# Decode attention: a new order of work units, and cache chunks loaded and used in two halves

## The chip, the cores and the metric

The kernel runs on one core of a Trainium2 chip. The metric is the device time of one execution in microseconds (us). The kernel before takes 1149 us (1149.11 median of 3 runs, 1147.62 to 1150.12).

## The reference, cut to what matters

Two layers of attention, each followed by a small MLP block, run over a batch of 8 rows with one new token each. Both attention layers read the same K and V caches.

```python
B, Sq, D = 8, 1, 448;  Hq, Hkv, Sk, Dh = 16, 8, 4096, 256

def _A_ref(x, k_cache, v_cache, wq, wo):
    q = (x @ wq)...                              # 16 heads
    k = jnp.repeat(k_cache, 2, axis=1)           # two q heads share one kv head
    v = jnp.repeat(v_cache, 2, axis=1)
    scores = jnp.einsum("bhqd,bhkd->bhqk", q, k) * (Dh ** -0.5)
    o = jnp.einsum("bhqk,bhkd->bhqd", softmax(scores), v)
    return o... @ wo

x = x + _A_ref(_layernorm(x), K, V, wq, wo)      # pass 0
x = x + _B_ref(_layernorm(x), w1, w2, w3, w4)    # per row, no mixing across rows
x = x + _A_ref(_layernorm(x), K, V, wq, wo)      # pass 1, same K and V
x = x + _B_ref(_layernorm(x), w1, w2, w3, w4)
```

## The kernel before: the parts that matter

Work is cut into units (pass, batch row, pair of kv heads). A unit has four K chunks and four V chunks of 1 MB. SBUF holds 15 places of 1 MB. Eleven of a row's 32 chunks, those of head pair 3 and three of pair 2, are *kept*: they are loaded and transposed in pass 0 and stay until pass 1 uses them. So 424 chunks are loaded for 512 uses. While all eleven are kept, four places are left for everything else.

```python
NC = 15
kept = [(GP-1, kv, n) for n in range(4) for kv in range(2)] + [(GP-2, 0, n) for n in range(3)]
LAG = 4                                    # V chunk j-4 is used after K chunk j
keep, free = [2, 3], [0, 1]                # head pairs with kept chunks, and without
tasks = [(0, 0, gp) for gp in free + keep] + [(0, 1, gp) for gp in free]
tasks += [(0, 2, free[0])]
for b in range(Bn):
    tasks += [(1, b, gp) for gp in keep[::-1]]
    if b + 1 < Bn:
        tasks += [(0, b + 1, gp) for gp in keep]
    if b == Bn - 2:
        tasks += [(1, Bn - 3, free[-1])]
    tasks += [(1, b, gp) for gp in (free[:-1] if b == Bn - 3 else free)]
    if b + 2 < Bn:
        tasks += [(0, b + 2, gp) for gp in (free[1:] if b == 0 else free)]

def emit_loads(most=None):                 # called after each use: a free place is loaded again
    while loads and places and ...:
        it = loads.pop(0); p = where[it] = places.pop(0)
        ...
        nc.sync.dma_start(dst[:], src)     # one DMA, 128 partitions x 8 KB

def transpose_k(t):                        # 16 rows of 1 KB per partition, in place
    for half in range(2):                  # a half is half of every row
        w = t[:].bitcast(U32).rearrange("p (y e w) -> p y e w", e=2, w=64)[:, :, half]
        nc.vector.transpose(w, w)

def scores(sc, t, x, qbd, gp):             # 32 matmuls, four column groups (k) side by side
    kv = t[:].rearrange("p (k t e i r) -> p k e r t i", k=4, t=4, e=4, r=2)
    for n in range(8):
        ...
        for k in range(4):
            nc.tensor.matmul(sc[32*k : 32*k + 8, 128*x : 128*x + 128], ...)
```

Beside this stream runs the *chain* of a row: softmax sums, output projection, MLP and the new q, cut into 30 small steps that are spread over the items between the row's last pass-0 unit and its first pass-1 unit.

Of the kernel before, what the change touches and what calls it, by code (L numbers as in the profile page):

```python
# [10 lines left out]
U32 = mybir.dt.uint32  # L11
# [6 lines left out]
def kernel(  # L18
# [27 lines left out]
    nc = tc.nc  # L46
    Bn, Sq, D = A_x.shape
# [13 lines left out]
    NC = 15  # L61
# [58 lines left out]
    sc_t = [ps_s.tile([128, 512], FP32, name=f"sc{n}") for n in range(2)]  # L120
# [337 lines left out]
    def claim(st):  # L458

        return st.setdefault("begun", 0) == 0 and st.update(begun=1) is None  # L460

    def last(b, st):
        yield from half(st["o"], st["z"], 0, OT2[:, :, :, b])
# [22 lines left out]
    keep = sorted({gp for gp, _, _ in kept})  # L486
    free = [gp for gp in range(GP) if gp not in keep]
    assert Bn > 2 and free == [0, 1] and GP == 4
    tasks = [(0, 0, gp) for gp in free + keep] + [(0, 1, gp) for gp in free]
# [2 lines left out]
    tasks += [(0, 2, free[0])]  # L492
    for b in range(Bn):
        tasks += [(1, b, gp) for gp in keep[::-1]]
        if b + 1 < Bn:
            tasks += [(0, b + 1, gp) for gp in keep]
        if b == Bn - 2:
            tasks += [(1, Bn - 3, free[-1])]
        tasks += [(1, b, gp) for gp in (free[:-1] if b == Bn - 3 else free)]
        if b + 2 < Bn:  # L500
            tasks += [(0, b + 2, gp) for gp in (free[1:] if b == 0 else free)]


    nk = 4 * len(tasks)
# [7 lines left out]
    def stays(it):  # L512
        n, kv, c = it
        return (tasks[n][2], kv, c) in kept
# [2 lines left out]


    places = list(range(NC))
    where = {}  # L520

    def emit_loads(most=None):
        n = 0
        while loads and places and n != most:
            it = loads.pop(0)
            p = where[it] = places.pop(0)
            if stays(it):
                where[tasks[it[0]][1:], it[1:]] = p
            t, kv, c = it
            _, b, gp = tasks[t]  # L530
            dst = slots[p]
            rows = (A_v_cache if kv else A_k_cache)[b, 2 * gp : 2 * gp + 2].rearrange(
                "g s d -> (g s) d"
            )
            if kv:
                src = rows.rearrange("(a p y) d -> a p (y d)", a=4, y=16)[c]
            else:
                src = rows.rearrange("(p x y) d -> x p (y d)", x=4, y=16)[c]
            nc.sync.dma_start(dst[:], src)  # L539
            n += 1  # L540

    def transpose_k(t):


        for half in range(2):
            w = t[:].bitcast(U32).rearrange("p (y e w) -> p y e w", e=2, w=64)[:, :, half]
            nc.vector.transpose(w, w)  # L547

    def scores(sc, t, x, qbd, gp):
        kv = t[:].rearrange("p (k t e i r) -> p k e r t i", k=4, t=4, e=4, r=2)  # L550
        for n in range(8):
            half, e2, par = n // 4, (n // 2) % 2, n % 2
            ep = 4 * e2 + 2 * par + half
            for k in range(4):
                nc.tensor.matmul(  # L555
                    sc[32 * k : 32 * k + 8, 128 * x : 128 * x + 128],
                    qbd[:, ep, gp].rearrange("p a h -> p (a h)"),
                    kv[:, k, 2 * half + e2, par],
                    start=(n == 0),
                    stop=(n == 7),  # L560
                )

    def exps(p_sb, sc, zall, gp):
        nc.scalar.activation(  # L564
# [68 lines left out]
    def run(g):  # L633
        while True:
            try:
                next(g)
            except StopIteration as e:
                return e.value
# [6 lines left out]
    def step(idx):  # L645

        for kind in ("chain", "last"):
            bank[0] = kind
            e = next((e for e in gens if e["kind"] == kind), None)
            if e is None:  # L650
                continue
            if e["n"] == 0:
                e["at"] = max(e["at"], idx)
            if e["n"] < e["of"] * (idx - e["at"] + 1) / max(e["until"] - e["at"], 1):
                e["n"] += 1
                if next(e["g"], gens) is gens:
                    gens.remove(e)
# [6 lines left out]
    for idx, it in enumerate(items):  # L664
        n, kv, c = it
        ps, b, gp = tasks[n]
        p = where[(b, gp), (kv, c)] if ps == 1 and stays(it) else where[it]
        slot = slots[p]
        final = (ps, b) == (1, Bn - 1)
        if kv == 0:  # L670
            if (ps, b) not in state:
                if ps == 1:
                    while (1, b) not in state:
                        step(10 * len(items))
                else:
                    state[0, b] = {}
            st = state[ps, b]
            if "q" not in st:
                qbd = work.tile([128, 8, GP, 4, 2], BF16, tag="qbd", bufs=3)
                run(spread_q(st["qT"][:] if ps == 1 else qT1[:, :, b], qbd))  # L680
                st["q"] = qbd
            if "o" not in st:
                z_t = chn.tile([128, GP], FP32, tag="zall", bufs=3)
                st["o"], st["z"] = o_banks[0], z_t
                o_banks.append(o_banks.pop(0))
                if final:
                    st["y"] = o_banks[0][:, 0:4].unsqueeze(2)
                    oc = st["o"][:, 0 : 2 * Hq].rearrange("p (j h) -> p j h", j=2)
            if not (ps == 1 and stays(it)):
                transpose_k(slot)  # L690
            step(idx)
            scores(sc_t[n % 2], slot, c, st["q"], gp)
            if c == 0 and n > 0:
                transpose_p(p_of.pop(n - 1))
            if c == 3:
                p_n = work.tile([128, 4, 32, 4], BF16, tag="p_sb", bufs=1)
                p_of[n] = p_n
                exps(p_n, sc_t[n % 2], st["z"], gp)
        else:
            st = state[ps, b]  # L700
            if n in p_of:
                transpose_p(p_of.pop(n))
            if final and gp in free and c == 1:
                rz_gp = run(z_cols(st["z"], [gp]))
            step(idx)
            if final and gp in free:
                pv_cols(oc, slot, c, gp)
                if c % 2 == 1:

                    u = c // 2  # L710
                    scale_o(oc, rz_gp, gp, u, OT2[:, :, :, b])
                    h0 = 8 * gp + 4 * u
                    run(
                        add_cols(
                            st["y"],
                            lambda i: OT2[:, i % 2, i // 2, b : b + 1],
                            wo_sb,
                            range(h0, h0 + 4),
                            1,
                            5,  # L720
                            first=claim(st),
                            stop=(gp == free[-1] and u == 1),
                        )
                    )
            else:
                pv(st["o"], slot, c, gp, begin=(ps, b) not in begun)
                begun.add((ps, b))
            if c == 3:
                done = pairs_done[ps, b] = pairs_done.get((ps, b), 0) + 1
                if done == 2 and ps == 0:  # L730
                    add_gen("chain", b, first_half(b, st), idx + 1, idx + 21, 9)
                elif done == 2:
                    add_gen("chain" if final else "last", b, first_last(b, st), idx + 1, idx + 13, 9)
                elif done == 4 and ps == 0:
                    add_gen("chain", b, chain(b, st), idx + 1, first_of[(1, b), 0] - 1, 30)
                elif done == 4 and not final:
                    add_gen("last", b, last(b, st), idx + 1, idx + (7 if b == Bn - 2 else 13), 6)
                    if b == Bn - 2:
                        add_gen("last", 0, rest(b, st), idx + 1, len(items) - 2, 21)
        if not (ps == 0 and stays(it)):  # L740
            if final and stays(it) and at_end is not None:

                if not at_end:
                    at_end, spare[:] = True, []
                spare.append(slot)
                if len(spare) == 2:
                    at_end = None
            else:
                places.append(p)
        emit_loads()  # L750
        step(idx)
    while gens:
# [12 lines left out]
    for q in range(4):  # L765
        for fc in range(4):
            w = 128 if fc < 3 else 64
            lo, hi = max(W * q, 128 * fc), min(W * q + W, 128 * fc + w)
            if lo < hi:
# [4 lines left out]
                    start=(lo == W * q),  # L774
                    stop=False,
                    skip_group_check=True,
                )
    for c in range(HC):
        for q in range(4):
# [4 lines left out]
                start=False,  # L784
                stop=(c == HC - 1),
# [38 lines left out]
```

## Time and profile before

| | before |
|---|---|
| time, median of 3 | 1149.11 us |
| bytes read | 455.15 MB |
| rate where loads are backed up | 419 to 420 GB/s |
| rate in the eight tight stretches | 371 to 403 GB/s |
| TensorE, VectorE busy | 61%, 48% |

From the page of the kernel before: busy time of the engines, the GB/s row of the 40 slices, the packets, the chain that ended last by engine, the costliest group of VectorE and of TensorE (after the bar: busy us, mean ns of one, then idle time before it and what ended it), and the load issues with their median time from issue to landing.

```profile
PE 705.3 (61%) x17177; PEld 514.0 (45%) x17177; DVE 548.2 (48%) x904; ACT 113.9 (10%) x234; POOL 15.6 (1%) x25
...
GB/s 352 375 420 420 407 385 399 418 412 383 414 420 400 385 399 419 420 403 406 409 420 420 400 400 413 420 420 387 402 412 420 408 371 412 420 410 355 410 420 153
DMA packets 68349, 457.52 MB, mean 398 GB/s; under 512 B 6999, under 2 KB 13030, under 8 KB 13542
...
DMA 69%; PE 13%; DVE 11%; SPq 3%; issue 2%; POOL 1%; ACT 0%; POOLq 0%; DVEq 0%; ACTq 0%
...
L547 DVE STREAM_TRANSPOSE slot<-slot 128x1024 uint32<-128x1024 uint32 x400 | 472.7, 1222 | 383.7 <-DMA slot<-in_A_k_cache_dram 375.0
L555 PE MATMUL sc<-slot,qbd 128*8 128x128 bf16 x8192 | 280.6, 286 | 345.6 <-DVE slot L547 287.2
...
slot<-in_A_v_cache_dram SPq DMA_DIRECT2D x224, 1024.0 KB, 12.3
slot<-in_A_k_cache_dram SPq DMA_DIRECT2D x200, 1024.0 KB, 16.4
```

TensorE, the busiest engine, is busy for 61% of the span, and the chain of waits is DMA. The GB/s row is the useful one: it reaches 420 and dips eight times. The table of engine time by stretch puts numbers on the dips. Its columns are the stretch, its length, each engine's busy us with its instructions, the granted TensorE clock, the DMA share and GB/s. First the eight dips:

```profile
130.00:180.00 50.00, 37.25 (x922) 28.45 (x914) 23.42 (x58) 4.10 (x10) 1.26 (x2) 1.00 0.99 381
250.00:290.00 40.00, 30.58 (x754) 23.30 (x749) 22.15 (x51) 3.46 (x8) 1.25 (x2) 0.50 0.99 382
360.00:420.00 60.00, 40.11 (x942) 29.42 (x945) 32.97 (x64) 5.56 (x12) 1.25 (x2) 0.50 0.99 384
500.00:560.00 60.00, 40.36 (x922) 29.80 (x923) 34.16 (x64) 4.49 (x12) 1.25 (x2) 0.50 1.00 403
640.00:700.00 60.00, 41.02 (x958) 30.59 (x962) 32.75 (x67) 5.02 (x10) 1.25 (x2) 0.50 1.00 397
770.00:830.00 60.00, 40.64 (x943) 29.30 (x934) 32.40 (x63) 5.53 (x12) 1.25 (x2) 0.50 1.00 396
910.00:950.00 40.00, 29.35 (x700) 22.63 (x704) 23.13 (x50) 2.30 (x6) 1.25 (x2) 0.50 0.98 372
1030.00:1080.00 50.00, 37.57 (x925) 28.62 (x922) 23.27 (x57) 4.89 (x11) 1.25 (x2) 0.54 0.98 371
```

and two of the stretches between them:

```profile
60.00:130.00 70.00, 35.56 (x802) 23.45 (x801) 34.44 (x38) 6.50 (x12) 0.00 (x0) 1.00 1.01 420
440.00:500.00 60.00, 35.15 (x779) 23.79 (x778) 29.04 (x30) 6.17 (x12) 0.00 (x0) 0.51 1.01 420
```

The dips last 420 us together with a mean of 387 GB/s; 420 × (1 − 387/420) = 33 us are lost in them. They are the stretches with eleven kept places full ("tight" below). What a place goes through there is in the timeline (start, length, engine, line, operation, count, idle before it and what ended it):

```profile
363.80 2.37 DVE L547 STREAM_TRANSPOSE slot<-slot 128x1024 uint32<-128x1024 uint32 x2 [2.60 <-DMA slot<-in_A_k_cache_dram]
365.10 0.60 PE L555 MATMUL sc<-slot,qbd 128*8 128x128 bf16 x16 [2.40 <-DVE slot L547]
366.22 0.60 PE L555 MATMUL sc<-slot,qbd 128*8 128x128 bf16 x16 [0.53 <-DVE zm L373]
366.86 0.33 SPq L539 DMA_DIRECT2D slot<-in_A_k_cache_dram  x1
```

VectorE waited for the K chunk to land. Two transposes take 2.37 us. Half of the scores follow each transpose, and 3.06 us after the first transpose began SyncE issues a load again (366.86 − 363.80).

### The profile page before, as it was taken

To read this page: it belongs to the slowest core of one execution; us is meant where nothing else is said; L and a number is where in the kernel's file an instruction comes from. 1 tells how busy PE (TensorE), PEld (TensorE's weight loads), DVE (VectorE), ACT (ScalarE), POOL (GpSimd) and SP (SyncE) were. 2 spreads that over 40 slices of the span, in tenths; PEclk is the share of its full clock that TensorE was granted. 3 is DMA by queue.
4 is the path that set the end of the run, shared out by engine and by line. 5 is a ranking of instruction groups with operands and counts; after the bars stand their busy time and mean duration, and the time that the engine had idled before them with its cause. 6 is when DMAs were issued, how large, how long until landed. Compare 5 with 4: busy or idle time off the path is not lost.

```text
span 1149.6 us, 36707 instructions
## 1 busy us (share of the span) xinstructions
PE 705.3 (61%) x17177; PEld 514.0 (45%) x17177; DVE 548.2 (48%) x904; ACT 113.9 (10%) x234; POOL 15.6 (1%) x25
## 2 busy tenths in 40 slices
PE   3144677457755667456764676646665576647787
PEld 2023455345533455344542454425443365425666
DVE  5145453455354544546254553445534553445352
ACT  0001011100110011001110101010011001100100
POOL 0000000000000000000000000000000000000000
PEclk9999997655655556555565557555575556555655
DMA  9999999999999999999999999999999999999993
GB/s 352 375 420 420 407 385 399 418 412 383 414 420 400 385 399 419 420 403 406 409 420 420 400 400 413 420 420 387 402 412 420 408 371 412 420 410 355 410 420 153
DMA packets 68349, 457.52 MB, mean 398 GB/s; under 512 B 6999, under 2 KB 13030, under 8 KB 13542
## 3 DMA queue, kind: packets, MB, share of 16 engines
q1 hardware_dynamic: 68198, 455.19, 98.0%
q8 instruction: 134, 2.20, 0.8%
q14 instruction: 17, 0.14, 0.0%
HBM read 455.15 MB, written 0.01 MB: 396 GB/s over the span
## 4 chain that ended last, share of the span: by engine, by line
DMA 69%; PE 13%; DVE 11%; SPq 3%; issue 2%; POOL 1%; ACT 0%; POOLq 0%; DVEq 0%; ACTq 0%
DMA slot<-in_A_k_cache_dram 62%; DVE slot L547 9%; DMA slot<-in_A_v_cache_dram 6%; PE sc L555 4%; PE o L596 3%; PE y_ps L318 2%; SPq L148 2%; PE q_ps L274 1%; DMA wq_sb<-in_A_wq_dram 1%; SPq L539 1%; PE o L610 1%; DVE qbd L300 1%; PE o L318 1%; PE h_ps L336 0%; PE misc L381 0%
## 5 line engine op out<-in xcount | busy, mean ns | idle before, releaser
L547 DVE STREAM_TRANSPOSE slot<-slot 128x1024 uint32<-128x1024 uint32 x400 | 472.7, 1222 | 383.7 <-DMA slot<-in_A_k_cache_dram 375.0
L555 PE MATMUL sc<-slot,qbd 128*8 128x128 bf16 x8192 | 280.6, 286 | 345.6 <-DVE slot L547 287.2
L555 PEld LDWEIGHTS <-qbd 128*8 128x8 bf16 x8192 | 194.5, 105 | 430.8 <-issue 298.6
L596 PE MATMUL o<-slot,ptw 128*8 128x256 bf16 x3968 | 242.8, 388 | 55.8 <-DMA slot<-in_A_v_cache_dram 33.9
L564 ACT ACTIVATE p_n<-sc 128x512 bf16<-128x512 f32 x64 | 84.7, 1323 | 780.6 <-PE sc L555 780.6
L596 PEld LDWEIGHTS <-ptw 128*8 128x8 bf16 x3968 | 107.9, 109 | 93.8 <-issue 45.0
L318 PEld LDWEIGHTS <-wo_sb 128*128 128x128 bf16 (+1 forms) x1600 | 64.8, 124 | 16.2 <-issue 15.6
L318 PE MATMUL y_ps<-OT,wo_sb 128*128 128x1 bf16 (+1 forms) x1280 | 55.5, 177 | 1.5 <-issue 1.5
L384 DVE RECIPROCAL rz<-misc 128x8 f32<-128x8 f32 (+1 forms) x33 | 6.4, 193 | 96.3 <-PE misc L381 96.3
L274 PEld LDWEIGHTS <-wq_sb 128*128 128x128 bf16 x1152 | 33.9, 104 | 19.1 <-issue 17.3
L274 PE MATMUL q_ps<-xb,wq_sb 128*128 128x1 bf16 (+1 forms) x1152 | 35.3, 166 | 11.4 <-DMA wq_sb<-in_A_wq_dram 3.6
L584 ACT CAST ptw<-misc 128x128 bf16<-128x128 f32 x64 | 17.5, 274 | 211.9 <-PE misc L577 159.4
L411 PEld LDWEIGHTS misc<-R,o_sb 128*128 128x128 f32 x124 | 25.9, 293 | 11.0 <-issue 11.0
L318 PEld LDWEIGHTS <-w_sb 128*128 128x128 bf16 (+1 forms) x630 | 25.7, 125 | 7.3 <-issue 5.2
L411 PE MATMUL misc<-R,o_sb 128*128 128x8 f32 x124 | 28.8, 343 | 0.0
L232 POOL TENSOR_TENSOR t<-t,nhalf 128x2 f32<-128x2 f32 (+1 forms) x17 | 10.7, 630 | 1075.8 <-DVE t L239 978.0
L318 PE MATMUL y_ps<-HT_t,w_sb 128*128 128x1 bf16 (+1 forms) x560 | 24.2, 177 | 0.5 <-DVE HT_t L359 0.5
L300 DVE TENSOR_SCALAR qbd<-misc,quad 128x64 bf16<-128x64 f32 x64 | 13.8, 278 | 22.0 <-PE misc L294 22.0
L381 PE MATMUL misc<-zm,one 128*128 128x8 f32 (+1 forms) x66 | 18.1, 348 | 6.7 <-ACT ptw L584 6.7
L336 PEld LDWEIGHTS <-w_sb 128*128 128x128 bf16 x560 | 17.2, 105 | 9.6 <-issue 9.2
L336 PE MATMUL h_ps<-xb,w_sb 128*128 128x1 bf16 (+1 forms) x560 | 17.9, 166 | 4.9 <-DVE xb L249 4.6
L381 PEld LDWEIGHTS misc<-zm,one 128*128 128x128 f32 x66 | 15.2, 287 | 11.9 <-ACT ptw L584 8.4
(92 smaller groups left out, 207.7 us busy)
## 6 DMA issues: line engine op xcount, KB each, us to landing
slot<-in_A_v_cache_dram SPq DMA_DIRECT2D x224, 1024.0 KB, 12.3
slot<-in_A_k_cache_dram SPq DMA_DIRECT2D x200, 1024.0 KB, 16.4
wo_sb<-in_A_wo_dram SPq DMA_DIRECT2D x1, 3584.0 KB, 26.6
wq_sb<-in_A_wq_dram SPq DMA_DIRECT2D x3, 1024.0 KB, 7.0
w_sb<-in_B_w_dram SPq DMA_DIRECT2D x1, 1568.0 KB, 12.8
w_sb<-in_B_w_dram SPq DMA_DIRECT2D x3, 448.0 KB, 26.8
wq_sb<-in_A_wq_dram SPq DMA_DIRECT2D x2, 256.0 KB, 10.0
w_sb<-in_B_w_dram SPq DMA_DIRECT2D x2, 112.0 KB, 9.0
```

The costliest lines, as they stand in the source:

```text
L148: nc.sync.dma_start(t[:, fc * cols : (fc + 1) * cols], src[fc * 128 : fc * 128 + 128, :])
L274: nc.tensor.matmul(q_ps[:, j * Hq + h, :], w, xbs(nb)[:, xi, :], start=(fc == 0), stop=(fc == 3),)
L300: nc.vector.tensor_scalar_mul(qbd[:, :, :, a, :], qs.rearrange("p e (f g u h) -> p (e f) u g h", f=2, u=2, h=2)[:, :, u], quad[:, a : a + 1],)
L318: nc.tensor.matmul(r, w[:, i, lo:hi], rhs(i), start=(first and fc == 0 and i == rows[0]), stop=(stop and i == rows[-1]), skip_group_check= ...
L336: nc.tensor.matmul(h_ps[:, c * nb : c * nb + nb], w, xbs(nb)[:, xi, :], start=(fc == 0), stop=(fc == 3),)
L381: nc.tensor.matmul(z_ps, ones, zm[:], start=True, stop=True)
L411: nc.tensor.matmul(ot_ps[:, j], o_sb[:, 128 * j : 128 * j + 128], R[:], start=True, stop=True)
L547: nc.vector.transpose(w, w)
L555: nc.tensor.matmul(sc[32 * k : 32 * k + 8, 128 * x : 128 * x + 128], qbd[:, ep, gp].rearrange("p a h -> p (a h)"), kv[:, k, 2 * half + e2, ...
L564: nc.scalar.activation(p_sb[:].rearrange("p t i x -> p x t i"), sc[:].rearrange("p (x t i) -> p x t i", x=4, t=4), ACT.Exp, scale=scale_ex ...
L584: nc.scalar.copy(ptw[:, :, :, 6:8], pt_ps.rearrange("p t k (a h) -> p a (t k) h", a=4),)
L596: nc.tensor.matmul(o_ps[32 * q : 32 * q + 8, 256 * (g // 4) : 256 * (g // 4) + 256], ptw[:, a, 4 * (y % 4) + y // 4, w : w + 8], v[:, y * ...
```

## The change

The intent: the load of a place begins when its last use ends, so use it sooner. A chunk is loaded as two DMAs of 8 rows per partition, and each half is transposed and scored as it lands. Since smaller loads cost something, only loads issued with 10 or more kept places full are parted. And for `b` = 1 to 4 in the list of tasks, one unit of row b moves ahead of the kept units of row b + 1, so that three units instead of four separate the two kept passes of row b + 1 and its tight stretch is shorter.

```diff
-        if b + 1 < Bn:
+        if b == Bn - 2:
             tasks += [(0, b + 1, gp) for gp in keep]
-        if b == Bn - 2:
-            tasks += [(1, Bn - 3, free[-1])]
-        tasks += [(1, b, gp) for gp in (free[:-1] if b == Bn - 3 else free)]
-        ...
+            tasks += [(1, Bn - 3, free[-1])] + [(1, b, gp) for gp in free]
+        elif b == Bn - 1:
+            tasks += [(1, b, gp) for gp in free]
+        else:
+            early = 0 < b < Bn - 3
+            tasks += [(1, b, free[0])] * early + [(0, b + 1, gp) for gp in keep]
+            tasks += [(1, b, gp) for gp in free[early : 1 if b == Bn - 3 else 2]]
+            ...
-            nc.sync.dma_start(dst[:], src)
+            if len(held) >= NC - 5:
+                parted.add(it)
+            for c0, c1 in [(0, 2048), (2048, 4096)] if it in parted else [(0, 4096)]:
+                nc.sync.dma_start(dst[:, c0:c1], src[:, c0:c1])
 # transpose_k: a half is now the first or last 8 rows
-            w = t[:].bitcast(U32).rearrange("p (y e w) -> p y e w", e=2, w=64)[:, :, half]
+            w = t[:].bitcast(U32)[:, 1024 * half : 1024 * half + 1024]
+            if not parts:
+                w = ...as before
 # scores: the first 8 rows are column groups 0 and 1, the last 8 are 2 and 3
+        rows = [(0, 1), (2, 3)] if parts else [(0, 1, 2, 3)]
+        for ks in rows:
+            for n in range(8):
+                ...
-            for k in range(4):
+                for k in ks:
```

So the new order shortens the tight stretches of rows 2 to 5 only (rows count from 0); elsewhere three units lay between the kept passes before, too.

More of the change, by code (lines that the diff above doesn't have):

```diff
@@ L494 @@
         tasks += [(1, b, gp) for gp in keep[::-1]]
-        if b + 1 < Bn:
+        if b == Bn - 2:
             tasks += [(0, b + 1, gp) for gp in keep]
-        if b == Bn - 2:
-            tasks += [(1, Bn - 3, free[-1])]
-        tasks += [(1, b, gp) for gp in (free[:-1] if b == Bn - 3 else free)]
-        if b + 2 < Bn:
-            tasks += [(0, b + 2, gp) for gp in (free[1:] if b == 0 else free)]
+            tasks += [(1, Bn - 3, free[-1])] + [(1, b, gp) for gp in free]
[5 more added lines that the diff above has]
+            tasks += [(1, b, gp) for gp in free[early : 1 if b == Bn - 3 else 2]]
+            if b + 2 < Bn:
+                tasks += [(0, b + 2, gp) for gp in (free[1:] if b == 0 else free)]
     nk = 4 * len(tasks)
@@ L519 @@
     places = list(range(NC))
-    where = {}
+    where, held, parted = {}, set(), set()
     def emit_loads(most=None):
@@ L528, in emit_loads @@
                 where[tasks[it[0]][1:], it[1:]] = p
+                held.add(p)
             t, kv, c = it
@@ L538, in emit_loads, with transpose_k, scores @@
                 src = rows.rearrange("(p x y) d -> x p (y d)", x=4, y=16)[c]
-            nc.sync.dma_start(dst[:], src)
+            if len(held) >= NC - 5:
+                parted.add(it)
+            for c0, c1 in [(0, 2048), (2048, 4096)] if it in parted else [(0, 4096)]:
+                nc.sync.dma_start(dst[:, c0:c1], src[:, c0:c1])
             n += 1
-    def transpose_k(t):
+    def transpose_k(t, parts):
         for half in range(2):
-            w = t[:].bitcast(U32).rearrange("p (y e w) -> p y e w", e=2, w=64)[:, :, half]
+            w = t[:].bitcast(U32)[:, 1024 * half : 1024 * half + 1024]
+            if not parts:
+                w = t[:].bitcast(U32).rearrange("p (y e w) -> p y e w", e=2, w=64)[:, :, half]
             nc.vector.transpose(w, w)
-    def scores(sc, t, x, qbd, gp):
+    def scores(sc, t, x, qbd, gp, parts):
         kv = t[:].rearrange("p (k t e i r) -> p k e r t i", k=4, t=4, e=4, r=2)
-        for n in range(8):
-            half, e2, par = n // 4, (n // 2) % 2, n % 2
-            ep = 4 * e2 + 2 * par + half
-            for k in range(4):
-                nc.tensor.matmul(
-                    sc[32 * k : 32 * k + 8, 128 * x : 128 * x + 128],
-                    qbd[:, ep, gp].rearrange("p a h -> p (a h)"),
-                    kv[:, k, 2 * half + e2, par],
-                    start=(n == 0),
-                    stop=(n == 7),
-                )
+        rows = [(0, 1), (2, 3)] if parts else [(0, 1, 2, 3)]
+        for ks in rows:
+            for n in range(8):
+                e4, par = n // 2, n % 2
+                ep = 4 * (e4 % 2) + 2 * par + e4 // 2
+                for k in ks:
+                    nc.tensor.matmul(
+                        sc[32 * k : 32 * k + 8, 128 * x : 128 * x + 128],
+                        qbd[:, ep, gp].rearrange("p a h -> p (a h)"),
+                        kv[:, k, e4, par],
+                        start=(n == 0),
+                        stop=(n == 7),
+                    )
     def exps(p_sb, sc, zall, gp):
@@ L689 @@
             if not (ps == 1 and stays(it)):
-                transpose_k(slot)
+                transpose_k(slot, it in parted)
             step(idx)
-            scores(sc_t[n % 2], slot, c, st["q"], gp)
+            scores(sc_t[n % 2], slot, c, st["q"], gp, it in parted)
             if c == 0 and n > 0:
@@ L749 @@
                 places.append(p)
+            held.discard(p)
         emit_loads()
```

## The prediction

> **What bounds the kernel now.** Loading. The chain of waits is DMA for 69% of the span, 62% of it K chunks. The core reads 455.15 MB. Where the queue stays backed up (60–130, 440–500, 720–770 us and five more stretches, table of engine time by stretch) it moves 419–420 GB/s: one 1 MB chunk per 2.48 us, as issue times in the timeline also show. At that rate all bytes take 1084 us. Of the remaining 65 us, about 8 are the start (weights), 18 the tail after the last load lands near 1131, and 33 lie in eight stretches (130–180, 250–290, 360–420, 500–560, 640–700, 770–830, 910–950, 1030–1080; 420 us) with a mean of 387 GB/s: 420 × (1 − 387/420) = 33 us.
>
> There eleven kept places leave four for everything else. A K chunk takes 5–8 us from issue to landing, 2.4 us for two transposes of 1.22 us, 1.1 us of scores, and only then is its place loaded again. The backlog ahead of a new load falls from about 17 us to 4.5–6 and the queue runs dry: most 8 KB packets still take 309 ns but some take microseconds. It is latency, not engine speed: the first stretch had the full granted clock (1.00) and lost as much as those at 0.50.
>
> **What the change does.**
> 1. Order. By walking the lists, b=1..4 go from four units to three between kept passes; the others already had three. Loads issued with all eleven kept places full fall from 221 to 177 of 424. But today's four-unit stretches lose no more (3.9 us each) than the three-unit ones (4.4): three units pack the chain's work tighter. I count −2 us.
> 2. Halves, for 217 chunks (96 K, 121 V). The first transpose runs while the second half lands, so transposes end about 1.2 us sooner. But scores now use two of four column groups at a time: 32 matmuls took 1.07 us at half clock; I estimate about 1.9, and the last 16 about 0.5 us longer. A K place comes free about 0.7 us sooner, a V place about 0.5. The page "TensorEngine Tiling (Array Packing)", Performance Considerations, gives up to 4× for four column tiles; here half is given up. I expect half of the dry time to go: −17 us.
> 3. Packets become 4 KB. Packets of 8192 B take 309 ns, of 3584 B 140, the fastest of 4096 B 159: two need 318, a second semaphore packet 9 more. So 2–3% more queue time, 0.05–0.09 us per parted chunk, 11–19 us if all counted; part falls into dry time. I count +8. "DMA: Bandwidth & Descriptors", Bandwidth, advises at least 1 MiB per DMA; halves are 0.5 MiB.
>
> Transposes, bytes and weights stay; SP issues 217 DMAs more (0.33 us each, off the path).
>
> **Sum.** 1149 − 2 − 17 + 8 = **1138 us**, range 1123–1153. Faster by over 2%: 0.12; within 2%: 0.85; slower: 0.03. Even with no dry time left, 1149 − 33 + 11 = 1127 is about the threshold.
>
> **What would show it.** Stretches at b=1..4 get shorter, with similar loss each. GB/s in tight stretches rises from 387 to 395–405, but parted loads top out near 410–414, not 420; about 27,000 packets of 8 KB remain beside 55,600 of 4 KB. PE busy on scores rises by 20–60 us; PE slices in tight stretches reach 9.
>
> **What would make it wrong.** Half packets that overlap better than their durations say (near 1125). PE: tight three-unit stretches are busy 6–8 tenths; slower scores could block pv, which waits in order behind them (1150+). Tracking that waits for both halves (then only the packet cost stays).

## More of the kernel before

With the new order 217 of the 424 loads are parted (96 K, 121 V); with the old order it would be 273 (124 K, 149 V).

## The result, and the profile after

The changed kernel takes 1159.88 us (median of 4, 1158.67 to 1161.93) beside 1149.61 us for the kernel before. The ratio is 1.0093 with a 95% interval of 1.0072 to 1.0114. The change made the kernel 0.9% slower; 1123 to 1153 us had been predicted.

The same lines of the page, for the changed kernel:

```profile
PE 747.0 (65%) x17177; PEld 559.2 (48%) x17177; DVE 551.6 (48%) x904; ACT 113.9 (10%) x234; POOL 15.7 (1%) x25
...
GB/s 351 376 419 419 408 374 408 419 406 379 405 420 418 395 352 420 420 416 395 374 420 421 413 380 379 419 420 407 380 386 419 411 386 400 418 412 381 406 418 158
DMA packets 99602, 457.57 MB, mean 395 GB/s; under 512 B 10472, under 2 KB 16503, under 8 KB 72567
...
DMA 42%; PE 19%; DVE 8%; issue 3%; ACT 1%; POOL 1%; POOLq 0%; SPq 0%; ACTq 0%; DVEq 0%
...
L557 DVE STREAM_TRANSPOSE slot<-slot 128x1024 uint32<-128x1024 uint32 x400 | 476.4, 1225 | 327.4 <-DMA slot<-in_A_k_cache_dram 323.5
L567 PE MATMUL sc<-slot,qbd 128*8 128x128 bf16 x8192 | 333.0, 283 | 309.3 <-DVE slot L557 260.6
...
slot<-in_A_v_cache_dram SPq DMA_DIRECT2D x242, 512.0 KB, 8.3
slot<-in_A_k_cache_dram SPq DMA_DIRECT2D x104, 1024.0 KB, 19.8
slot<-in_A_v_cache_dram SPq DMA_DIRECT2D x103, 1024.0 KB, 19.8
slot<-in_A_k_cache_dram SPq DMA_DIRECT2D x192, 512.0 KB, 8.1
```

The shares of the chain that ended last add up to 74% only: in this profile it could not be followed back to the start. The same kernel was run once more (below, "the change again"), and there it is whole:

```profile
DMA 57%; PE 24%; DVE 11%; issue 3%; SPq 3%; ACT 1%; POOL 1%; POOLq 0%; ACTq 0%; DVEq 0%
```

So the chain of waits has moved from DMA (69% to 57%) towards TensorE (13% to 24%). Scores keep TensorE busy for 333 us instead of 281. VectorE waits less for K chunks (323.5 us instead of 375.0), but with the new order alone it is 343.3, so this says little about the halves. The dips are still there, and longer. The eight stretches of the changed kernel in which the rate falls:

```profile
130.00:180.00 50.00, 42.28 (x898) 32.96 (x901) 23.80 (x59) 4.08 (x10) 1.26 (x2) 1.00 1.02 388
260.00:300.00 40.00, 33.00 (x778) 25.67 (x774) 17.05 (x44) 5.45 (x12) 1.26 (x2) 0.55 1.00 380
370.00:440.00 70.00, 53.57 (x1208) 41.92 (x1211) 32.88 (x71) 7.34 (x16) 1.25 (x2) 0.55 1.00 381
510.00:570.00 60.00, 46.05 (x962) 35.55 (x961) 31.30 (x67) 5.49 (x12) 1.26 (x2) 0.56 1.01 385
640.00:710.00 70.00, 50.39 (x1089) 38.91 (x1093) 35.47 (x70) 6.15 (x15) 1.25 (x2) 0.53 1.00 383
790.00:860.00 70.00, 52.94 (x1217) 41.40 (x1217) 34.42 (x72) 7.36 (x16) 1.26 (x2) 0.58 1.00 386
920.00:980.00 60.00, 47.89 (x1127) 36.88 (x1127) 29.04 (x61) 5.76 (x13) 1.25 (x2) 0.64 1.02 393
1040.00:1090.00 50.00, 43.60 (x968) 34.58 (x962) 22.66 (x55) 5.47 (x12) 1.25 (x2) 0.55 1.01 389
```

They last 470 us with a mean of 386 GB/s: 470 × (1 − 386/420) = 38 us lost, against 33. TensorE is busy for 369.7 of these 470 us (79%); before it was 296.9 of 420 (71%). The four reordered stretches, the third to the sixth, came down from 384–403 to 381–386 GB/s; by the same sum they lose 23 us instead of 14. In the other four, where only the halves are new, the loss fell from 19 to 15 us. And parted loads with plenty of loads in the queue, at the entry to such stretches, run at 409 to 410 GB/s, where the stretches above with loads backed up ran at 420:

```profile
230.00:250.00 20.00, 10.37 (x198) 6.83 (x194) 9.77 (x9) 1.85 (x4) 0.00 (x0) 0.50 1.02 409
370.00:390.00 20.00, 11.67 (x218) 8.34 (x217) 11.31 (x17) 1.87 (x4) 0.00 (x0) 0.50 1.03 410
```

The DMA share is above 1, so nothing is idle there; 4 KB packets are slower for the same bytes. The packet records of the trace give a median of 159 ns for 4096 B and 312 ns for 8192 B. By the median over parted loads that were queued behind others, 1 MB takes 2.56 us instead of 2.48.

So there were four suspects: packets, the queue's depth (more DMAs for the same bytes), slower scores, and the order.

### The profile page after: what moved, and what is told of

The parts are those of the page before. It is cut to its first block, busy times and chain, and to the rows that moved or that the text cites. A ratio compares the mean times of both kernels' runs of the same rounds, so it can differ in the third digit from the quotient of the medians.

```text
span 1157.8 us, 37174 instructions
## 1 busy us (share of the span) xinstructions
PE 747.0 (65%) x17177; PEld 559.2 (48%) x17177; DVE 551.6 (48%) x904; ACT 113.9 (10%) x234; POOL 15.7 (1%) x25
## 4 chain that ended last, share of the span: by engine, by line
DMA 42%; PE 19%; DVE 8%; issue 3%; ACT 1%; POOL 1%; POOLq 0%; SPq 0%; ACTq 0%; DVEq 0%
DMA slot<-in_A_k_cache_dram 24%; DMA slot<-in_A_v_cache_dram 19%; PE sc L567 6%; DVE slot L557 6%; PE y_ps L318 3%; PE o L608 3%; PE q_ps L274 1%; PE misc L411 1%; ACT p_n L576 1%; PE o L622 1%; PE misc L381 1%; PE o L318 1%; PE misc L589 0%; POOL t L232 0%; PE st L212 0%
## 5 line engine op out<-in xcount | busy, mean ns | idle before, releaser
L557 DVE STREAM_TRANSPOSE slot<-slot 128x1024 uint32<-128x1024 uint32 x400 | 476.4, 1225 | 327.4 <-DMA slot<-in_A_k_cache_dram 323.5
L567 PE MATMUL sc<-slot,qbd 128*8 128x128 bf16 x8192 | 333.0, 283 | 309.3 <-DVE slot L557 260.6
L567 PEld LDWEIGHTS <-qbd 128*8 128x8 bf16 x8192 | 245.3, 105 | 395.0 <-issue 271.3
L608 PE MATMUL o<-slot,ptw 128*8 128x256 bf16 x3968 | 252.7, 383 | 51.1 <-DMA slot<-in_A_v_cache_dram 28.7
L608 PEld LDWEIGHTS <-ptw 128*8 128x8 bf16 x3968 | 113.1, 107 | 89.1 <-issue 41.1
```

The source lines that it names most:

```text
L567: nc.tensor.matmul(sc[32 * k : 32 * k + 8, 128 * x : 128 * x + 128], qbd[:, ep, gp].rearrange("p a h -> p (a h)"), kv[:, k, e4, par], star ...
L608: nc.tensor.matmul(o_ps[32 * q : 32 * q + 8, 256 * (g // 4) : 256 * (g // 4) + 256], ptw[:, a, 4 * (y % 4) + y // 4, w : w + 8], v[:, y * ...
```

## The experiments

Sixteen experiments ran, all with five rounds. "Old order" is that of the kernel before. Every kernel passed the comparison with the reference. After the first row, each four rows ran together on one chip, with the kernel before in the same rounds; a ratio compares within its own rounds, and two ratios of different groups are compared across chips.

| run | order | loads parted | use | ratio to before | 95% interval |
|---|---|---|---|---|---|
| the change | new | 217 | halves, two groups | 1.0093 | 1.0072–1.0114 |
| order only | new | 0 | whole | 1.001 | 0.9985–1.0036 |
| halves only | old | 273 | halves, two groups | 1.0041 | 1.0017–1.0065 |
| loads only | old | 273 | whole | 1.0105 | 1.0077–1.0133 |
| compute only | old | 0 | halves, two groups | 1.012 | 1.0095–1.0144 |
| the change again | new | 217 | halves, two groups | 1.0098 | 1.0072–1.0124 |
| four groups | old | 273 | halves, four groups late | 1.0042 | 1.0016–1.0067 |
| rows dealt, old | old | 273 | halves, four groups early | 1.023 | 1.0201–1.0259 |
| rows dealt, new | new | 217 | halves, four groups early | 1.028 | 1.0252–1.0309 |
| half depth | old | 0, plus 273 tiny DMAs | whole | 1.000 | 0.998–1.002 |
| small packets | old | 0, but 273 in 4 KB runs | whole | 1.0145 | 1.0126–1.0165 |
| four groups, new | new | 217 | halves, four groups late | 1.0055 | 1.004–1.0069 |
| late K | old | 100 K | halves, four groups late | 0.9966 | 0.9949–0.9982 |
| K only | new | 96 K | halves, two groups | 1.003 | 1.0008–1.0053 |
| V only | new | 121 V | halves | 1.002 | 0.9985–1.0054 |
| late K, new | new | 72 K | halves, four groups late | 1.004 | 1.0016–1.0063 |
| late K, two groups | old | 100 K | halves, two groups | 0.9951 | 0.9928–0.9973 |

### Order and halves apart

Theory A was that the order does the harm, since time was lost in the reordered stretches. Rival B was that the halves do it. The first kernel takes the new list of tasks alone, the second all of the change but that list.

> Only the new unit order, loads whole. Theory A (the order does the harm: in the changed kernel the time lost beyond 2.48 us per chunk rose by about 2.2 us in each of the four reordered stretches, from 5.3 to 7.5 us, and fell by 2 us in all in the other four): about 1157 us, ratio 1.006 to 1.009. Rival B (the halves do the harm, by packets and slower scores): 1146 to 1150 us, ratio at or under 1.000.

> Only the halves, in the old order; 273 chunks are then parted instead of 217. Theory A (order): 1144 to 1149 us, ratio 0.996 to 1.000. Rival B (halves): 1157 to 1162 us, ratio 1.007 to 1.011, as in the changed kernel or a little more. If neither alone costs anything, the harm is the two together: halves slow the PE where the new order packs its work.

Order alone took 1151.84 us (ratio 1.001, no difference that is clear of the noise). Halves alone took 1155.48 us (1.0041). Neither theory got its number. Together they cost 1.0093 and 1.0098 in two measurements, so about half a per cent exists only where both are there. It is rather more, since the new order also parts 56 chunks fewer (217 instead of 273), which by the cost per parted chunk found below is worth 2 to 3 us (an estimate).

### Loading in halves without using halves, and the reverse

```diff
 # loads only
-                transpose_k(slot, it in parted)
+                transpose_k(slot, False)
-            scores(sc_t[n % 2], slot, c, st["q"], gp, it in parted)
+            scores(sc_t[n % 2], slot, c, st["q"], gp, False)
 # compute only
-            for c0, c1 in [(0, 2048), (2048, 4096)] if it in parted else [(0, 4096)]:
+            for c0, c1 in [(0, 4096)]:
```

> Old order, chunks loaded in two halves, but transposes and scores as before (they need both halves). It shows what 4 KB packets cost without the gain from early use. If packets are paid in full (2.57 against 2.48 us for 273 chunks) the time rises by 15 to 20 us, ratio 1.013 to 1.018. If the dry time takes up most of it: 1150 to 1154 us.

> Old order, whole loads, but transposes and scores by halves with two column groups for the 124 K chunks. It shows what the slower scores cost alone. PE busy on scores rises by about 60 us. If in-order PE work is what empties the queue, 1153 to 1160 us; if only latency from landing counts, about 0.5 us later per K place, 1149 to 1152 us.

Loads only took 1163.56 us (1.0105), between its two expectations: per parted chunk (1.0105 − 1) × 1150.9 us / 273 = 0.044 us, about half of the 0.08 us that a parted chunk takes longer in a full queue. Compute only took 1165.12 us (1.012), more than both of its expectations. The group of score matmuls of the second, from its page:

```profile
L563 PE MATMUL sc<-slot,qbd 128*8 128x128 bf16 x8192 | 361.3, 285 | 296.9 <-DVE slot L553 252.3
```

The same 8192 matmuls keep TensorE busy 81 us longer than before (280.6), because two column groups at a time take longer than four. This costs about 14 us, although TensorE is idle for a third of the span: a K place is issued again 3.79 us after its chunk landed, against 3.30 us before (how these are worked out is told below). So both parts of the halves cost over 1%, and using halves early gives back most of it: 1.0105 and 1.012 would make 1.0225 if they added, and together they are 1.0041. Set against loads only, with the same loads in the same rounds, early use with its slower scores gains 7 us (1.0105 to 1.0041).

### The change again, and two ways to keep four column groups

```diff
 # four groups: halves loaded and transposed, scores after both transposes
-            scores(sc_t[n % 2], slot, c, st["q"], gp, it in parted)
+            scores(sc_t[n % 2], slot, c, st["q"], gp, False)
 # rows dealt: row y is (t, k) instead of (k, t), so half the rows reach all four groups
-        kv = t[:].rearrange("p (k t e i r) -> p k e r t i", k=4, t=4, e=4, r=2)
-        for ks in rows: ... for k in ks:
-                        sc[32 * k : 32 * k + 8, 128 * x : 128 * x + 128], ... kv[:, k, e4, par]
+        kv = t[:].rearrange("p (t k e i r) -> p k e r t i", k=4, t=4, e=4, r=2)
+        for t0, t1 in [(0, 2), (2, 4)] if parts else [(0, 4)]: ... for k in range(4):
+                        sc[32 * k : 32 * k + 8, 128 * x + 32 * t0 : 128 * x + 32 * t1], ... kv[:, k, e4, par, t0:t1]
-                ptw[:, a, 4 * (y % 4) + y // 4, ...
+                ptw[:, a, y, ...
```

> The changed kernel again, beside the next three on one chip: ratio 1.007 to 1.011 as on record. Order alone gave 1.001 and halves alone 1.0041; if both simply added, 1.005. A ratio clear above that means the order costs more where scores are slow.

> Old order; loads and transposes by halves, but the scores of a chunk run with four column groups after both transposes. Theory S (the two-group scores cost about 14 us of the 1.2% that halved compute alone lost): PE busy on scores back near 280 us and 1141 to 1147 us, ratio 0.992 to 0.997. Rival P (the PE time of scores does not matter; packets and waiting cost it): 1153 to 1158 us, ratio 1.002 to 1.006.

> Old order; halves as in the change, but rows are dealt to the column groups so that each half holds rows of all four: twice as many score matmuls in a parted chunk, of 64 columns each, on four groups. Theory S: scores' PE busy between 280 and 330 us, 1138 to 1146 us, ratio 0.990 to 0.996, a little better than with scores after both transposes, as the first half is scored early. If the extra matmuls are bound by issue and cost as much as two groups did: 1153 to 1158 us.

> The changed kernel with that same dealing of rows to four column groups, new order. Theory S with the order harmful only through PE work: the order then costs nothing, within 0.3% of the old-order version, ratio 0.989 to 0.996. If the order hurts by itself when loads are halved (fewer items to spread the chain's steps over), it stays 0.4% or more above the old-order version.

The change repeated at 1162.34 us (1.0098). Four groups took 1156.69 us (1.0042), the same as halves with two groups (1.0041): in the old order, scoring early gains what two groups cost. Theory S had expected under 0.997 and fell.

Rows dealt took 1177.48 us (1.023) and 1183.32 us (1.028), the worst of all, far above theory S. The new order is again half a per cent above the old here, in the same rounds and although the scores are fast in both (busy 283.7 and 286.5 us): the order does not hurt through slow scores alone. What TensorE waited for, from the waits of the old-order version, shows what rows dealt cost (total us, times, longest):

```profile
PE sc L562 <- issue: 89.1, 52, 4.1
```

In the kernel before the same entry is 23.0 us. "issue" is time in which the engine waits for nothing that the profile shows. The trace has the instruction queue's DMAs too, 16 KB each. Their number went from 134 to 165, as parted K chunks now have 64 matmuls instead of 32. In this run 88 gaps of over 0.6 us, in which TensorE neither multiplied nor loaded weights, ended 1.1 to 1.6 us after such a fetch had ended (18 would by chance), and 85 of them stood within the same 16 of 256 positions of TensorE's instruction stream; in the kernel before it is 31 (14 by chance) and 23. That points to instruction fetch. It was found from the trace and not tested by a run of its own. For the question here the lesson is only that more, smaller matmuls are no free way out.

### Packets or depth

Each load takes one of eight semaphores in turn, and a new load waits for the one eight before it. With two DMAs per chunk the queue therefore holds half the bytes. Theory Q made this the cost of halved loads, theory P the 4 KB packets. One kernel has the depth without the packets, the other the packets without the depth; both are in the old order with whole use.

```diff
 # half depth
             nc.sync.dma_start(dst[:], src)
+            if it in parted:
+                i = len(parted) % 8
+                nc.sync.dma_start(tiny[:, 4 * i : 4 * i + 4], A_x...[0:1, 0:4])
 # small packets: one DMA, runs of 4 KB (rows in another order)
+            if it in parted:
+                src = ...rearrange("(a e p y) d -> a p e (y d)", a=4, e=2, y=8)[c]   # K alike, "(p e x y)"
+                nc.sync.dma_start(dst[:].rearrange("p (e d) -> p e d", e=2), src)
```

> Old order, whole loads and whole use as before, but a DMA of 8 bytes is issued after each of the 273 loads that would be parted. The trace shows never more than 8 DMAs in flight (the loads use eight semaphores in turn), so with two DMAs per chunk only four chunks, 10 us of work, can wait in the queue instead of eight, 20 us. Theory Q (this shallower queue is what halved loads cost): 1157 to 1163 us, ratio 1.006 to 1.011. Theory P (4 KB packets cost it): 1149 to 1153 us, ratio 0.999 to 1.002.

> Old order, one DMA per chunk and whole use as before, but the 273 chunks are fetched in runs of 4 KB instead of 8 KB (rows in another order, so the result is wrong on purpose). Theory P (packets): ratio 1.007 to 1.012, as with loads alone in halves (1.0105). Theory Q (queue depth): 0.999 to 1.003. If both share it, each shows about half.

Half depth took 1149.81 us: ratio 1.000. The depth did fall, as its issues show (KB each, median us from issue to landing; before, 12.3 and 16.4):

```profile
slot<-in_A_v_cache_dram SPq DMA_DIRECT2D x224, 1024.0 KB, 9.8
slot<-in_A_k_cache_dram SPq DMA_DIRECT2D x200, 1024.0 KB, 8.9
```

It costs nothing, and neither do 273 more DMAs for SyncE to issue. Small packets took 1168.12 us: ratio 1.0145, more than theory P expected. (Its page counts 83,430 packets under 8 KB, the kernel before 13,542. Its rows pair K with the wrong V. The comparison with the reference passed all the same, so this was no visible error.) Theory Q fell and theory P stood. (1.0145 − 1) × 1150.7 us / 273 = 0.061 us per chunk, three quarters of the 0.08 us that a parted chunk takes longer in a full queue; loads only gave 0.044, on another chip and with the rows in their usual order. So between a quarter and half of the longer queue time is absorbed, and the rest is paid.

### The order where the scores are not slow, and a version meant to be better

The first has the change with the "four groups" edit. The second, in the old order, parts only K chunks and only from the sixth load with eleven kept places full, when the queue has run low:

```diff
+            if len(held) < NC - 5:
+                tight[0] = 0
+            elif len(held) >= NC - 4:
+                tight[0] += 1
-            if len(held) >= NC - 5:
+            if kv == 0 and tight[0] > 5:
                 parted.add(it)
```

> The new order with halved loads and transposes, but scores on four column groups after both transposes (old order gave 1.0042). If the new order costs only where slow scores fill the PE (the changed kernel: 1.0098 against 1.0041 for halves in the old order), this gives 1.002 to 1.006, and with 217 instead of 273 parted chunks perhaps 1.001. If the order costs by itself once the queue is shallow or packets small: 1.008 to 1.012.

> A version meant to be better: old order, whole loads while the queue is still deep; only K chunks, and only from the sixth load on with eleven kept places full, come in halves (100 chunks), scores on four groups. If the loss is packets and depth, both fall by more than half and the early transposes stay: 1140 to 1148 us, ratio 0.991 to 0.998. If halving buys nothing in the dry part: 1.000 to 1.004.

Four groups in the new order took 1156.99 us (1.0055), against 1.0042 in the old order: no clear cost of the order, though the 56 chunks fewer may hide 2 to 3 us of it. Late K took 1147.13 us (0.9966), within its expectation.

### K or V, and the order once more

> The changed kernel, but V chunks load whole; 96 K chunks stay parted, with two-group scores. Packets at 0.06 us per parted chunk, as measured with small packets alone, would save 121 x 0.06 = 7 us. If V halves gain nothing: 1152 to 1156 us, ratio 1.001 to 1.005. If V halves do gain 0.5 us per place as predicted, it is no better than the changed kernel: 1.008 to 1.011.

> The changed kernel, but K chunks load whole and are used as before; 121 V chunks stay parted. Packets cost 7 us and nothing is gained if V halves are useless: 1.005 to 1.008. If V halves pay for their packets: 0.997 to 1.002. Together with the K version it should account for the changed kernel's excess of 1.009 to 1.010.

> The better version (only late K chunks in halves, four-group scores; 0.9966 in the old order) in the new order. If the order costs nothing by itself: 0.994 to 0.999. If it costs where loads are parted at all: 1.000 to 1.004.

> The better version in the old order, but with the two-group early scores of the change for its 100 K chunks. If slow scores cost what early scoring gains (as in the old order with all chunks parted): 0.995 to 0.999, equal. If slow scores cost by themselves, 1.000 to 1.004.

The edits are the condition above with `kv == 0`, with `kv == 1`, the late-K kernel with the new task list, and the late-K kernel with the scores of the change. K only took 1155.45 us (1.003), V only 1152.85 us (1.002); neither carries the loss alone, and their sum is half of it. The two expectations contradict each other here: read from the K version, V halves cost what their packets cost; read from the V version, they about pay for them (1.002, where packets alone would give 1.006 by 121 × 0.061 = 7 us). The costs do not add; they seem to grow where both sorts are parted, though with these intervals that is barely clear of the noise. Late K in the new order took 1156.18 us (1.004), the upper end of its second expectation, that the order costs where loads are parted at all: with four-group scores the order still cost 0.7%. So the idea that the order hurts only through slow scores, which the four-groups pair had supported, does not hold, as the two kernels with rows dealt had already shown. Late K with two groups took 1146.30 us (0.9951), the fastest kernel of all (not clear of late K's 0.9966).

### What the semaphore records show

The trace holds every increment of the load semaphores. A half has landed with the sixteenth increment after its issue. From these I worked out, for loads with eleven kept places full, when the first transpose of a K chunk begins. The two halves of a parted chunk land about 1.35 us apart (mean; the median is 1.28).

| kernel | first transpose begins, median | mean, from the last landing |
|---|---|---|
| before | 0.02 us after the chunk landed | +0.19 us |
| order only | 0.02 us after the chunk landed | +0.23 us |
| halves only, old order | 0.10 us after its first half landed | −0.77 us |
| the change | 1.00 us after its first half landed | −0.29 us |
| four groups, new order | 0.69 us after its first half landed | −0.37 us |
| late K | 0.09 us after its first half landed | −0.65 us |
| late K, new order | 0.78 us after its first half landed | −0.10 us |

In the old order VectorE is ready when the first half lands, and transposes begin 0.96 us sooner than before (0.19 + 0.77). In the new order it is late by most of the 1.35 us and only 0.52 us are gained (0.23 + 0.29). With late K the order does the same: 0.09 us becomes 0.78. (In the two late-K rows not every chunk is parted; for a whole chunk its only landing counts.) The timeline of the changed kernel in a reordered stretch shows what VectorE is late for:

```profile
404.78 0.17 DVE L354 TENSOR_SCALAR g_t<-h_ps 128x14 f32<-128x14 f32 x1 [1.84 <-PE h_ps L336]
404.99 0.17 DVE L355 SCALAR_TENSOR_TENSOR g_t<-g_t,h_ps 128x14 f32<-128x14 f32 x1
405.19 0.17 DVE L356 SCALAR_TENSOR_TENSOR g_t<-g_t,h_ps 128x14 f32<-128x14 f32 x1
405.64 0.17 DVE L359 SCALAR_TENSOR_TENSOR HT_t<-g_t 128x14 bf16<-128x14 f32 x1 [0.28 <-ACT g_t L357]
405.73 2.37 DVE L557 STREAM_TRANSPOSE slot<-slot 128x1024 uint32<-128x1024 uint32 x2
```

The halves of this chunk landed at 403.45 and 405.20 by the semaphores. VectorE stood idle for 1.84 us until TensorE had done an MLP step of the chain, went through four such steps of its own, and both transposes then ran without a wait. Compare the chunk shown of before, which VectorE waited 2.60 us for. Of the 73 K chunks that the changed kernel loads with eleven kept places full, 55 had their first transpose begin more than 0.1 us after their first landing, 79 us late in all. In 44 of these us VectorE stood idle, most of them (some 33) until a matmul step of the chain on TensorE was done; in 30 it ran steps other than K transposes, and in 4 it still transposed another chunk. With halves only it is 45 of 101 chunks, 54 us late and 20 of them idle.

The release of places follows. For loads issued with eleven kept places full and no more than 3 MB on their way, a place is issued again after its last landing (means; waits for a kept place are left out):

| kernel | K place | V place |
|---|---|---|
| before | 3.30 us | 2.40 us |
| order only | 3.40 us | 2.69 us |
| halves only, old order (first half / second half) | 1.89 / 2.91 us | 2.38 / 2.99 us |
| the change (first half / second half) | 2.88 / 3.76 us | 2.92 / 3.48 us |

In the changed kernel the two halves of a K place come free at the same time as before on average (3.32 us), and those of a V place 0.8 us later (3.20 against 2.40), of which the order alone makes 0.3. In the old order a K place comes free 0.9 us sooner (2.40 against 3.30); that gain is what the new order takes away. Late K shows it too: 2.83 / 3.26 us in the old order, 3.75 / 4.22 us in the new.

## Why the prediction was wrong

1. **What bounds the kernel: right.** Loading does, and the loss sits in the eight tight stretches. Order, halves and packets all act there.
2. **Order, "I count −2 us": small error alone, wrong in combination.** Alone it cost nothing that is clear of the noise (1.001). Its reason, "three units pack the chain's work tighter", fits the late transposes, but I did not carry it to step 2, where the order removes the gain: halves alone are 1.0041, with the order 1.0093 and 1.0098.
3. **Halves, "I expect half of the dry time to go: −17 us": this is the step that failed.** It rested on "A K place comes free about 0.7 us sooner, a V place about 0.5". In the changed kernel the K place comes free no sooner and the V place 0.8 us later. In the old order, with 273 parted chunks, early use is worth 7 us net of the slower scores, set against loads only (1.0105 to 1.0041), or 12 us, set against small packets (1.0145). In the new order almost nothing is left: by an estimate from the same two runs, 217 × 0.044 = 10 to 217 × 0.061 = 13 us of packets and 1 us of order leave 0 to −3 us to reach the measured 11 us (1.0096 mean of two). So the step was off by 14 us or more, most of the 22 us between 1138 and 1160. What it had overlooked is that VectorE transposes in program order behind the chain's steps, so that it is not free when the first half lands.
4. **Packets, "I count +8": the mechanism was right and the size somewhat too small.** By the same estimate it is 10 to 13 us. "Part falls into dry time" holds, but the part is smaller than I took: 0.044 to 0.061 us of the 0.08 us are paid per parted chunk, where +8 us for 217 chunks meant 0.037.
5. **Slower scores.** I had counted "0.5 us longer" in the release of one place. Alone, on 124 K chunks, they cost 1.2% (compute only), with a K place released 0.49 us later (3.79 against 3.30): that size was right, and its price in the whole time was not seen. The Trainium skill's page "TensorEngine Tiling (Array Packing)", Performance Considerations, gives 4× for column tiles of 32; giving up half of it raised the scores' busy time from 280.6 to 361.3 us for 124 of 200 loaded K chunks. Four late groups and two early groups then came out equal.
6. **"What would show it" was mostly right and did not help.** Parted loads top out at 409–410 GB/s, scores' busy time rose by 52 us, slices of TensorE reach 9, and the packet counts came as said (26,880 of 8 KB, 55,680 of 4 KB). The rate in tight stretches was predicted to rise to 395–405 and fell to 386.
7. **Of "What would make it wrong",** "tracking that waits for both halves" did not happen: with halves only, 82% of the first transposes in tight stretches began before the second half had landed. "Slower scores could block pv, which waits in order behind them" named waiting in order on TensorE as the danger; the trace shows it on VectorE.

What stays open: why late K halves cost 0.7% more in the new order even with fast scores, while all chunks in halves with four groups cost there hardly more than in the old order (1.0055 and 1.0042); the 56 chunks fewer explain only a part. The late start of transposes behind the chain is shown in the traces; that it accounts for the whole difference is not, since no run moved the chain's steps away from the tight stretches and kept the order. Nor is it settled why V places gain so little even in the old order: the first half is issued no sooner on average (2.38 against 2.40 us), though by the medians it is (1.81 against 2.38).

## What to carry to other kernels

In these runs cutting a load in two gained where the engine that uses it was waiting when the first half landed, and not where that engine came late; look at what that engine does in those microseconds before counting a gain, and check it again after any reordering that packs other in-order work into the same stretch. Half or more of what smaller packets cost in a full queue was paid in the whole time, so part few loads, where the wait is real: 100 late K chunks gave 0.995 to 0.997, all 273 gave 1.004. And two effects of one change that share an engine are not to be added up as if they were apart.

## What the Trainium skill lacked or had wrong

- "DMA: Bandwidth & Descriptors", Specifications, gives 512 B as the minimum transfer for line rate. That row alone makes 4 KB packets look free. Here they still cost against 8 KB ones: two of 159 ns against one of 312 ns, 2.56 against 2.48 us per 1 MB, and 1.0 to 1.45% of the whole time for 273 chunks. The page names a fixed cost per packet further down, but gives no rate for packets of these sizes.
- The same page, Bandwidth, gives the rule of at least 1 MiB per DMA, from DMAs issued by GpSimd, and says nothing there of the runs inside one. Here the length of the contiguous runs mattered: 273 tiny DMAs added beside whole loads cost nothing (1.000), and 4 KB runs cost no less in 1 MB DMAs (1.0145) than in DMAs of 0.5 MB (1.0105). DMAs of 0.5 MB with 8 KB runs were not tried, so the rule itself is not tested.
- "Runtime: NRT & Kernel Launch", Instruction fetch mechanics, has crossings of 16 KiB blocks "mostly hidden". With more and shorter matmuls they appear not to be: in the old-order kernel with rows dealt 88 gaps of TensorE ended 1.1 to 1.6 us after a fetch of 16 KB had ended, 85 of them at one place modulo 256 instructions, beside 165 such fetches, with TensorE's "issue" waits at 89.1 us for the scores instead of 23.0. In the kernel before it was 23 beside 134 fetches, which agrees with the page.
- No page that I read gives how far apart one DMA's engines finish. Here the first and last semaphore increment of one 1 MB load were 2.4 us apart (median of the loads issued with eleven kept places full in the kernel before; 2.6 over all its loads), about as long as the load's own share of the queue, 2.48 us.
